# Routing attention and a mixer MLP: score groups of three key chunks instead of two, one PSUM bank for the small products

## The chip, the core and the metric

The kernel runs on one core of a Trainium2 chip. The metric is the device time of one execution in microseconds (us). The core's engines run side by side, each through its own list of instructions in order, and wait for each other by semaphores: TensorE (PE, matrix products; PEld is its weight load), VectorE (DVE), ScalarE (ACT), GpSimd (POOL) and SyncE (SP, which issues most DMA transfers). Products of PE land in PSUM, eight banks of 128 partitions by 2 KB (512 f32 numbers each); from there DVE or ACT reads them. SBUF is the larger working memory.

## The reference

What is computed, cut to what matters (B=4 batches, H=8 heads, S=768 positions, D=64, 16 clusters; the mixer has d_tok=256 and d_ch=1536):

```python
q_assign = argmax(einsum('bhsd,hcd->bhsc', q_n, c_n), axis=-1)
k_assign = argmax(einsum('bhsd,hcd->bhsc', k_n, c_n), axis=-1)
mask = q_assign[:, :, :, None] == k_assign[:, :, None, :]
scores = where(mask, scale * matmul(q, k.transpose(0, 1, 3, 2)), -1e9)
attn = exp(scores - max(scores, axis=-1, keepdims=True))
attn = attn / (sum(attn, axis=-1, keepdims=True) + 1e-09)
x = matmul(attn, v)                      # heads side by side: (B, S, 512)
h = maximum(x.transpose(0, 2, 1) @ w_tok1, 0) @ w_tok2
u = x + h.transpose(0, 2, 1)
out = u + maximum(u @ w_ch1, 0) @ w_ch2
```

`q_n`, `k_n` and `c_n` are the vectors divided by their norms.

## The kernel before

**Attention** works on pairs of heads: `NPAIR` = 16 pairs (batch b, heads 2f and 2f+1), counted by g. For one pair the 768 queries are two halves of 384 (`HS`, qh = 0, 1), and the 768 keys are six chunks of 128 (`NJ`). A group m is one half of the queries against two chunks of keys, so a pair has `GROUPS` = 6 groups and the loop at L745 runs over 96 of them, with five more iterations to drain. In the loop, `g, s = divmod(m, GROUPS)`: s is the place of the group within its pair.

For a group, `scores` (L352) computes for each chunk and each of the two heads a bf16 product of one-hot cluster vectors (`ohT`, which puts a large negative number where clusters differ) and adds the f32 product of keys and queries (`qkT`, the two halves of an f32 product are two instructions each). The two heads use two halves of the array's rows and run at the same time. One chunk fills a tile `sc` of two PSUM banks; ACT turns it into `ex` by an exponential (L367). `add_up` (L370) adds the `ex` tiles of a half on DVE into `sum`. `values` (L382) multiplies `ex` by the value vectors into `av` (one bank), and at the end of a half ACT copies it to `avT`.

Around them stand small products, all in tiles of the pool `ps_w` (three banks, tag "w"):

- `turn` (DVE transposes of the next pair's keys and queries into `qkT`), `route_products` (PE, `pr`), `route` (DVE: `sim`, `mx`, `oh`, in L310 to L316), and `route_turn` (PE transposes `po`, read by ACT into `ohT`): they prepare pair g+1 while pair g runs.
- `half_sums` (PE, `den`), `half_reciprocals` (DVE: `dent`, read from `den`, and `rcps`), `half_turn` (PE transposes `px` of `avT`) and `half_out` (DVE, reads `px` and writes `x`): they finish a half. They are issued 2, 3, 3 and 4 iterations after the half's last group.

The order of every engine's instructions is the order in which the program calls these functions; nothing reorders them. One iteration calls, in this order: `half_out` of group m-4, `add_up` of m-1, `scores` of m, `values` of m-2, one of the steps for the next pair (by s), the load of pair g+2 (s = 1), a weight step, `half_sums`, `half_reciprocals`, `half_turn`.

A **weight step** (`weight_steps`, L166) loads one piece of a weight matrix by SP, has ACT compute two helper tiles (`wh`, `wup`) of the piece before it and DVE and POOL round the one before that (L205 to L222). One is taken every `WEVERY` = 4 iterations.

**After attention** the token mixer (`tok1`, `tok2`, the list `ends`) and the channel mixer (`ch1_chunk`, `ch2_chunk`) run on PE nearly without a gap. The channel mixer keeps running products in PSUM tiles with the tags X and Z (`ps_m`, two buffers of each, opened where the score banks are closed) and Y (one tile of `ps_w`). `turn_u` (L526) transposes u for it, eight calls with four tiles `pt` of `ps_w`, each read by an ACT copy (L538). `fits` (L666) checks whether the fast path's assumptions hold; if not, `general` recomputes everything.

PSUM during attention: three banks `ps_w`, one `ps_av`, two tiles `sc` of two banks. Afterwards: three `ps_w`, one `ps_av`, four `ps_m`.

Of the kernel before, what the change touches and what calls it, by code (L numbers as in the profile page):

```python
# [17 lines left out]
C = 16  # L18
P = 128
# [11 lines left out]
QP = P // NQ  # L31
NPAIR = B * NF

GROUPS = NJ
WEVERY = 4
SM_SCALE = 0.125


# [8 lines left out]
def kernel(  # L47
# [35 lines left out]
    def pool(name, bufs, stack=None, **kw):  # L83
        return (stack or fast).enter_context(
            tc.tile_pool(name=name, bufs=bufs, reuse_waits="tile", **kw)
        )

    ps_w = pool("ps_w", 3, space=PSUM)
    ps_av = pool("ps_av", 1, space=PSUM)
    ps_sc_stack = fast.enter_context(ExitStack())  # L90
    ps_sc = pool("ps_sc", 2, ps_sc_stack, space=PSUM)

    xpool = pool("xpool", 1)
    wc1pool = pool("wc1pool", 1)
# [144 lines left out]
    def centroids_norm(cen):  # L239
        sq = rsmall.tile([P, D], F32, name="censq")  # L240
        ss = rsmall.tile([P, 1], F32, name="ss")
        nc.vector.tensor_tensor(out=sq, in0=cen, in1=cen, op=ALU.mult)
        nc.vector.reduce_sum(out=ss, in_=sq, axis=AX.X)

        lo = rsmall.tile([P, 1], F32, name="lo")
        nc.vector.tensor_scalar_max(out=lo, in0=ss, scalar1=float(2.0**-100))
        nrm = rsmall.tile([P, 1], F32, name="nrm0")
        nc.vector.tensor_scalar(
            out=nrm.bitcast(I32), in0=lo.bitcast(I32), scalar1=0.5, scalar2=float(0x1FBD1DF5),
            op0=ALU.mult, op1=ALU.add,  # L250
        )
        for it in range(3):
            rr = rsmall.tile([P, 1], F32, name="rr")
            nc.vector.reciprocal(out=rr, in_=nrm)
            tw = rsmall.tile([P, 1], F32, name="tw")
            nc.vector.scalar_tensor_tensor(
                out=tw, in0=ss, scalar=rr, in1=nrm, op0=ALU.mult, op1=ALU.add
            )
            nrm = rsmall.tile([P, 1], F32, name="nrm")
            nc.vector.tensor_scalar(  # L260
                out=nrm, in0=tw, scalar1=0.5, scalar2=(1e-6 if it == 2 else 0.0),
                op0=ALU.mult, op1=ALU.add,
            )
        rden = rsmall.tile([P, 1], F32, name="rden")
        nc.vector.reciprocal(out=rden, in_=nrm)
        cn = rsmall.tile([P, 2, D], F32, name="cn")
        for i in range(2):
            nc.vector.tensor_scalar_mul(out=cn[:, i], in0=cen, scalar1=rden)
        pc = ps_w.tile([P, H * C], F32, tag="w", name="pc")
        nc.tensor.transpose(out=pc, in_=cn.rearrange("p i d -> p (i d)"), identity=ident)  # L270
        nc.vector.tensor_copy(out=cnT, in_=pc)
        nc.vector.memset(cnd, 0.0)
        for i in range(2):
            rows = slice(i * D, (i + 1) * D)
            nc.vector.tensor_copy(
                out=cnd[rows, :, i], in_=cnT.rearrange("p (f i c) -> p f i c", f=NF, i=2)[rows, :, i]
            )


    def turn(g, kinds=(1, 0)):  # L280
# [3 lines left out]
        for a in kinds:  # L284
# [2 lines left out]
                in_=st["qk"][:, a].rearrange("p j i d -> p (j i d)"),  # L287
            )

    def route_products(g, a0=0, a1=2):  # L290

        st, f = state[g], g % NF
        pr = ps_w.tile([P, a1 - a0, NJ, QP], F32, tag="w", name="pr")
        for i in range(NQ):
            rows = slice(i * QP, (i + 1) * QP)
            nc.tensor.matmul(  # L296
                pr[rows], lhsT=cnd[:, f].rearrange("p i c -> p (i c)"),
                rhs=st["T"][:, a0:a1, :, rows].rearrange("p a j r -> p (a j) r"),
                start=True, stop=True,
            )  # L300
        st["pr"] = pr
# [20 lines left out]
    def route_turn(g, a):  # L322

        st, oh = state[g], ohs[g % 2]
        if a == 1:  # L330
            st["ohT"] = qktp.tile([P, 2, NJ, P], BF16, name="ohT")
        po = ps_w.tile([P, NJ, P], BF16, tag="w", name="po")
        for j in range(NJ):
            nc.tensor.transpose(out=po[:, j], in_=oh[:, a, j], identity=identb)  # L334
        if a == 0:
            if g == 0:
                nc.vector.tensor_copy(out=st["ohT"][:, 0], in_=po)  # L337
            else:
                nc.scalar.copy(out=st["ohT"][:, 0], in_=po)
        else:  # L340
            nc.scalar.activation(
                out=st["ohT"][:, 1], in_=po, func=ACT.Copy, scale=BIG, bias=-BIG,
                accum_out=cells[:, g : g + 1],
            )


    def split(m):

        g, s = divmod(m, GROUPS)
        return g, s // (GROUPS // 2), 2 * (s % (GROUPS // 2))  # L350

    def scores(m):  # L352
        g, qh, j0 = split(m)
        st = state[g]
        js = slice(HJ * qh, HJ * qh + HJ)
        scs = [ps_sc.tile([P, 2, 512], F32, name="sc") for _ in range(2)]
        for src, start in ((st["ohT"], True), (st["T"], False)):
            for i in range(2):
                for h in range(2):
                    rows = slice(h * D, (h + 1) * D)  # L360
                    nc.tensor.matmul(  # L361
                        scs[i][:, h, 0:HS], lhsT=src[rows, 1, j0 + i], rhs=src[rows, 0, js],
                        start=start, stop=not start,
                    )
        for i in range(2):
            ex = work.tile([P, 2, HS], F32, name="ex")
            nc.scalar.activation(out=ex, in_=scs[i][:, :, 0:HS], func=ACT.Exp, scale=SM_SCALE)  # L367
            st["ex", qh, j0 + i] = ex

    def add_up(m):  # L370
        g, qh, j0 = split(m)
        st = state[g]
        e = [st["ex", qh, j0 + i] for i in range(2)]
        if j0 == 0:
            acc = st["sum", qh] = sums.tile([P, 2, HS], F32, name="sum")
            nc.vector.tensor_tensor(out=acc, in0=e[0], in1=e[1], op=ALU.add)
        else:
            acc = st["sum", qh]
            for i in range(2):
                nc.vector.tensor_tensor(out=acc, in0=acc, in1=e[i], op=ALU.add)  # L380

    def values(m):  # L382
        g, qh, j0 = split(m)
        st = state[g]
        if j0 == 0:
            st["av"] = ps_av.tile([P, HS], F32, name="av")
        for j in (j0, j0 + 1):
            ex = st.pop(("ex", qh, j))
            for h in range(2):
                nc.tensor.matmul(  # L390
                    st["av"][h * D : (h + 1) * D], lhsT=st["va"][:, h, j], rhs=ex[:, h],
                    start=(j == 0), stop=(j == NJ - 1),
                )
        if j0 == NJ - 2:
            st["avT", qh] = sums.tile([P, HJ, P], F32, name="avT")
            nc.scalar.copy(out=st["avT", qh].rearrange("p j t -> p (j t)"), in_=st.pop("av"))

# [128 lines left out]
    def turn_u(b, n):  # L526
# [3 lines left out]
            pools["uTs"] = pools["u"].tile([P, 3, NF // 2, HS], F32, name="uTs")  # L530
        uT, uTs = pools["uT"], pools["uTs"]
        for f in range(NF):
            pt = ps_w.tile([P, HJ, P], F32, tag="w", name="pt")
            for i in range(HJ):
                nc.tensor.transpose(  # L535
                    out=pt[:, i], in_=xs[b][:, HJ * n + i, f * P : (f + 1) * P], identity=ident
# [14 lines left out]
    def chunk(n, product, done):  # L551


        def ptile(tag):
            if tag == "Y":
                return ps_w.tile([P, n], F32, tag="w", name="pY")
            return pools["ps_m"].tile([P, n], F32, tag=tag, name="p" + tag)

        X = ptile("X")
# [182 lines left out]

        return m // HALF if 0 <= m < last and m % HALF == HALF - 1 else None

    for m in range(last + 5):  # L745
        g, s = divmod(m, GROUPS)
        if half_at(m - 4) is not None:
            half_out(half_at(m - 4))
        if 1 <= m <= last:
            add_up(m - 1)  # L750
        if m < last:
            scores(m)
        if m == last:
            ps_sc_stack.close()
        if 2 <= m < last + 2:
            values(m - 2)
        if g < NPAIR - 1:
            if s == 0:
                turn(g + 1)
            elif s == 1:  # L760
                route_products(g + 1)
            elif s == 2:
                route(g + 1)
            elif s == 3:
                route_turn(g + 1, 1)
            elif s == 4:
                route_turn(g + 1, 0)
        if s == 1 and g + 2 < NPAIR:
            load(g + 2)
        if m == last - GROUPS:  # L770
# [1 line left out]
            routing.close()  # L772
            W["ch2"] = pool("wc2pool", 1, side="right").tile([P, NCT, DM], F32, name="wc2")
            weights = list(weight_steps(stage, W, ("ch2",)))
        if (m % WEVERY == 0 if m < last - GROUPS else m % 2 or m > last) and weights:
            weights.pop(0)()
        if half_at(m - 2) is not None:
            half_sums(half_at(m - 2))
        if half_at(m - 3) is not None:
            half_reciprocals(half_at(m - 3))  # L780
            half_turn(half_at(m - 3))
        if m >= last:
            if m == last:
                pools["ps_m"] = pool("ps_m", 2, space=PSUM)
            for _ in range(2):
                if ends:
                    ends.pop(0)()
    assert not state
    attention.close()
    pools["wsums"] = pool("wsums", 1, side="right")  # L790
# [238 lines left out]
```

## Time and profile before

| | us |
|---|---|
| median of 4 runs | 915.97 |
| the runs | 915.4 to 917.05 |
| the profiled execution | 915.2 |
| its span, first to last instruction | 913.4 |
| first `sc` block begins at | 14.68 |
| last pair of heads begins at | 347.74 |
| channel mixer begins at | 457.86 |

| stretch (us) | PE busy | DVE busy | ACT busy | granted clock |
|---|---|---|---|---|
| 34.3 to 347.7, pairs 2 to 15 | 313.40 | 242.79 | 182.53 | 1.00 |
| 368.6 to 457.9, token mixer | 89.30 | 51.38 | 18.71 | 1.00 |
| 457.9 to 913.4, channel mixer | 445.81 | 178.93 | 79.19 | 0.99 |

The profile is one execution. A group line has the source line, the engine, the operation, the tile written and the tiles read, how many there were, and then busy time, mean length of one, and idle time ahead of them with what ended it. In a timeline, each row has the start and the length in us of a run of like instructions, and in brackets how long the engine had been idle and what released it. Ends of matmuls are modelled, and consecutive ones overlap.

### The profile page before, as it was taken

How to read it: one execution, taken by the hardware profiler on the slowest of the kernel's cores; microseconds unless marked ns; L12 is line 12 of the kernel's file. 1: busy time of each engine (PE TensorE's matmuls, PEld its weight loads, DVE VectorE, ACT ScalarE, POOL GpSimd, SP SyncE). 2: the span in 40 equal slices, each digit the busy share in tenths (PEclk: the TensorE clock that was granted, in tenths of full speed). 3: DMA queues.
4: the chain of work that ended last, by engine and by line, in shares of the span. 5: the costliest groups of instructions: out<-in, count | busy, mean ns of one | idle time of the engine just before them, and what ended most of it. 6: DMA issues, size and time to landing. Idle time of an engine off the chain costs nothing.

```text
span 913.4 us, 11598 instructions
## 1 busy us (share of the span) xinstructions
PE 899.0 (98%) x4594; PEld 527.7 (58%) x4594; DVE 506.2 (55%) x851; ACT 307.2 (34%) x515; POOL 48.5 (5%) x40
## 2 busy tenths in 40 slices
PE   7999999999999999999999899999999999999997
PEld 3444444444444444444457668677686876858676
DVE  6778777878787765358554244343443334433342
ACT  3655565656565555232120021211212112130210
POOL 1011000101010100123000000000000000000000
PEclk9999999999999999999999999999999999999999
DMA  9553435353534200122000001000010000100001
GB/s 162 117 100 64 98 84 100 82 95 86 92 89 70 88 1 1 47 92 70 0 1 0 1 0 47 24 1 1 0 47 24 0 1 5 54 12 1 1 12 61
DMA packets 112830, 41.76 MB, mean 46 GB/s; under 512 B 101632, under 2 KB 105728, under 8 KB 112768
## 3 DMA queue, kind: packets, MB, share of 16 engines
q1 hardware_dynamic: 109632, 40.55, 19.5%
q10 hardware_dynamic: 3136, 0.39, 0.3%
q8 instruction: 38, 0.62, 0.3%
q14 instruction: 24, 0.20, 0.1%
HBM read 34.64 MB, written 6.29 MB: 45 GB/s over the span
## 4 chain that ended last, share of the span: by engine, by line
PE 98%; DMA 1%; DVE 0%; issue 0%; ACT 0%
PE sc L361 18%; PE av L390 15%; PE pX L596 14%; PE pX L647 14%; PE pZ L647 7%; PE pZ L596 7%; PE ph L463 5%; PE pu L472 5%; PE pY L647 3%; PE pY L596 3%; PE px L425 2%; PE po L334 2%; PE pr L296 1%; PE den L406 1%; PE pt L535 1%; DMA qk<-in_k_dram 1%
## 5 line engine op out<-in xcount | busy, mean ns | idle before, releaser
L367 ACT ACTIVATE ex<-sc 128x768 f32<-128x768 f32 x192 | 145.2, 808 | 116.5 <-PE sc L361 116.5
L380 DVE TENSOR_TENSOR sum<-sum,ex 128x768 f32<-128x768 f32 x128 | 132.9, 1038 | 31.1 <-ACT ex L367 22.6
L390 PE MATMUL av<-ex,va 128*64 128x384 f32 x768 | 145.1, 499 | 0.0
L361 PE MATMUL sc<-qkT 64*128 64x384 f32 x768 | 139.5, 482 | 0.0
L390 PEld LDWEIGHTS av<-ex,va 128*64 128x64 f32 x768 | 46.6, 136 | 86.5 <-issue 82.7
L361 PEld LDWEIGHTS sc<-qkT 64*128 64x128 f32 x768 | 70.5, 187 | 31.4
L596 PE MATMUL pX<-uT,wc 128*128 128x384 f32 x192 | 68.8, 495 | 1.6 <-issue 1.6
L604 ACT COPY p<-pX 128x384 f32<-128x384 f32 x24 | 11.4, 475 | 153.0 <-PE pX L596 153.0
L596 PEld LDWEIGHTS pX<-uT,wc 128*128 128x128 f32 x192 | 36.7, 193 | 26.7 <-issue 3.3
L361 PE MATMUL sc<-ohT 64*128 64x384 bf16 x384 | 48.2, 328 | 1.3 <-DVE ohT L337 0.6
L222 POOL TENSOR_TENSOR wc<-wT,wup 128x512 int32<-128x512 int32 x24 | 35.2, 1468 | 257.6 <-DVE wT L215 149.0
L431 DVE TENSOR_TENSOR x<-px,rcps 128x384 f32<-128x384 f32 x32 | 17.8, 558 | 47.9 <-PE px L425 46.7
L463 PE MATMUL ph<-x,wt 128*128 128x512 f32 x96 | 42.1, 594 | 0.0
L472 PE MATMUL pu<-h,wt 128*128 128x512 f32 x96 | 42.0, 592 | 0.0
L489 DVE TENSOR_TENSOR x<-pX,x 128x256 f32<-128x256 f32 x24 | 10.2, 424 | 53.0 <-PE pX L647 53.0
L489 DVE TENSOR_TENSOR c<-pZ,u 128x384 f32<-128x384 f32 x24 | 13.4, 558 | 46.8 <-PE pZ L596 46.8
L647 PE MATMUL pX<-w2s,hA 128*128 128x256 f32 x144 | 35.4, 382 | 0.5 <-DVE x L489 0.5
L489 DVE TENSOR_TENSOR hA<-pY,p 128x384 f32<-128x384 f32 x24 | 13.4, 557 | 40.4 <-PE pY L596 40.4
L647 PE MATMUL pX<-wc,hA 128*128 128x256 f32 x144 | 35.0, 379 | 0.0
L647 PE MATMUL pZ<-w2s,hS 128*128 128x256 f32 x144 | 35.0, 379 | 0.0
L647 PE MATMUL pY<-wc,hA 128*128 128x256 f32 x144 | 35.0, 379 | 0.0
L647 PE MATMUL pX<-w2s,hS 128*128 128x256 f32 x144 | 35.0, 379 | 0.0
(115 smaller groups left out, 1218.8 us busy)
## 6 DMA issues: line engine op xcount, KB each, us to landing
raw<-in_moe_w_ch_dram SPq DMA_DIRECT2D x24, 512.0 KB, 4.1
qk<-in_k_dram SPq DMA_DIRECT2D x64, 96.0 KB, 4.5
va<-in_v_dram SPq DMA_DIRECT2D x16, 384.0 KB, 3.3
out_dram<-x SPq DMA_DIRECT2D x24, 256.0 KB, 2.0
qk<-in_q_dram SPq DMA_DIRECT2D x60, 96.0 KB, 3.6
raw<-in_moe_w_tok_dram SPq DMA_DIRECT2D x3, 512.0 KB, 5.7
raw<-in_moe_w_tok_dram SPq DMA_DIRECT2D x4, 384.0 KB, 3.8
qk<-in_q_dram ACTq DMA_DIRECT2D x4, 96.0 KB, 4.3
```

The source lines that it names most:

```text
L222: nc.gpsimd.tensor_tensor(out=dst.bitcast(I32), in0=T, in1=up, op=ALU.add)
L334: nc.tensor.transpose(out=po[:, j], in_=oh[:, a, j], identity=identb)
L361: nc.tensor.matmul(scs[i][:, h, 0:HS], lhsT=src[rows, 1, j0 + i], rhs=src[rows, 0, js], start=start, stop=not start,)
L367: nc.scalar.activation(out=ex, in_=scs[i][:, :, 0:HS], func=ACT.Exp, scale=SM_SCALE)
L380: nc.vector.tensor_tensor(out=acc, in0=acc, in1=e[i], op=ALU.add)
L390: nc.tensor.matmul(st["av"][h * D : (h + 1) * D], lhsT=st["va"][:, h, j], rhs=ex[:, h], start=(j == 0), stop=(j == NJ - 1),)
L425: nc.tensor.transpose(out=px[:, i], in_=avT[:, i], identity=ident)
L463: nc.tensor.matmul(pf, lhsT=W["tok1"][:, j, t * P : (t + 1) * P], rhs=xs[b][:, j], start=(j == 0), stop=(j == NJ - 1),)
L472: nc.tensor.matmul(pu, lhsT=W["tok2"][:, t, j], rhs=h1s[b][:, t], start=(t == 0), stop=(t == NT - 1))
L489: nc.vector.tensor_tensor(out=dst, in0=a, in1=b, op=ALU.add)
L596: nc.tensor.matmul(psum, lhsT=A[a][:, k, c * P : (c + 1) * P], rhs=R[r][:, k], start=start and k == 0, stop=k == 1, skip_group_check=not s ...
L647: nc.tensor.matmul(psum, lhsT=h2[a][:, k, i * P : (i + 1) * P], rhs=Bw[w][:, 3 * part + k], start=start and k == 0, stop=k == 2, skip_grou ...
```

## The change

Groups have three chunks of keys (`NG` = 3), so a pair has four groups and the loop 64, with three iterations to drain. The score tiles take three times two banks; `ps_w` has one bank, which all small products share, apart from those of the first pair (`wtile` with g = 0) and `pc`, which use score tiles. `values` runs one group behind `scores` instead of two. The order in the loop is new, a weight step comes every third iteration, and after attention the tiles `pt` and `pY` are in `ps_m` with the tag Y (two buffers). In an iteration, `half_sums` and the first `route_turn` stand between `scores` and `values`; `half_turn`, `route_products` and the second `route_turn` stand behind `values`; `turn` and `route` come ahead of `add_up`. The helper `wtile` is called only by `route_products` and `route_turn`.

```diff
-GROUPS = NJ
-WEVERY = 4
+NG = 3
+GROUPS = 2 * NJ // NG
+WEVERY = 3
...
-    ps_w = pool("ps_w", 3, space=PSUM)
+    ps_w = pool("ps_w", 1, space=PSUM)
     ps_av = pool("ps_av", 1, space=PSUM)
     ps_sc_stack = fast.enter_context(ExitStack())
-    ps_sc = pool("ps_sc", 2, ps_sc_stack, space=PSUM)
+    ps_sc = pool("ps_sc", NG, ps_sc_stack, space=PSUM)
...
+    def wtile(g, shape, dt, name):
+
+        if g == 0:
+            return ps_sc.tile(shape, dt, tag="sc", name=name)
+        return ps_w.tile(shape, dt, tag="w", name=name)
...
-        scs = [ps_sc.tile([P, 2, 512], F32, name="sc") for _ in range(2)]
+        scs = [ps_sc.tile([P, 2, 512], F32, tag="sc", name="sc") for _ in range(NG)]
         for src, start in ((st["ohT"], True), (st["T"], False)):
-            for i in range(2):
+            for i in range(NG):
...
         if j0 == 0:
             acc = st["sum", qh] = sums.tile([P, 2, HS], F32, name="sum")
             nc.vector.tensor_tensor(out=acc, in0=e[0], in1=e[1], op=ALU.add)
-        else:
-            acc = st["sum", qh]
-            for i in range(2):
-                nc.vector.tensor_tensor(out=acc, in0=acc, in1=e[i], op=ALU.add)
+            e = e[2:]
+        acc = st["sum", qh]
+        for ex in e:
+            nc.vector.tensor_tensor(out=acc, in0=acc, in1=ex, op=ALU.add)
...
-        for j in (j0, j0 + 1):
+        for j in range(j0, j0 + NG):
...
-            pt = ps_w.tile([P, HJ, P], F32, tag="w", name="pt")
+            pt = pools["ps_m"].tile([P, HJ, P], F32, tag="Y", name="pt")
...
         def ptile(tag):
-            if tag == "Y":
-                return ps_w.tile([P, n], F32, tag="w", name="pY")
             return pools["ps_m"].tile([P, n], F32, tag=tag, name="p" + tag)
...
-    for m in range(last + 5):
+    for m in range(last + 3):
         g, s = divmod(m, GROUPS)
-        if half_at(m - 4) is not None:
-            half_out(half_at(m - 4))
+        more = g < NPAIR - 1
+        if half_at(m - 3) is not None:
+            half_out(half_at(m - 3))
+        if more and s == 0:
+            turn(g + 1)
+        if more and s == 1:
+            route(g + 1)
         if 1 <= m <= last:
             add_up(m - 1)
         if m < last:
             scores(m)
         if m == last:
             ps_sc_stack.close()
-        if 2 <= m < last + 2:
-            values(m - 2)
-        if g < NPAIR - 1:
-            if s == 0:
-                turn(g + 1)
-            elif s == 1:
-                route_products(g + 1)
-            elif s == 2:
-                route(g + 1)
-            elif s == 3:
-                route_turn(g + 1, 1)
-            elif s == 4:
-                route_turn(g + 1, 0)
+            pools["ps_m"] = pool("ps_m", 2, space=PSUM)
+        if half_at(m - 2) is not None:
+            half_sums(half_at(m - 2))
+            half_reciprocals(half_at(m - 2))
+        if more and s == 2:
+            route_turn(g + 1, 1)
+        if 1 <= m <= last:
+            values(m - 1)
+        if half_at(m - 2) is not None:
+            half_turn(half_at(m - 2))
+        if more and s == 0:
+            route_products(g + 1)
+        if more and s == 2:
+            route_turn(g + 1, 0)
         if s == 1 and g + 2 < NPAIR:
             load(g + 2)
...
-        if (m % WEVERY == 0 if m < last - GROUPS else m % 2 or m > last) and weights:
+        if m < last - GROUPS:
+            n = m % WEVERY == 0 or m == 1
+        else:
+            n = m % 2 if m < last else 2
+        for _ in range(min(n, len(weights))):
             weights.pop(0)()
-        if half_at(m - 2) is not None:
-            half_sums(half_at(m - 2))
-        if half_at(m - 3) is not None:
-            half_reciprocals(half_at(m - 3))
-            half_turn(half_at(m - 3))
         if m >= last:
-            if m == last:
-                pools["ps_m"] = pool("ps_m", 2, space=PSUM)
-            for _ in range(2):
-                if ends:
-                    ends.pop(0)()
+            for _ in range(3):
+                ends.pop(0)()
```

More of the change, by code (lines that the diff above doesn't have):

```diff
@@ L268, in centroids_norm @@
             nc.vector.tensor_scalar_mul(out=cn[:, i], in0=cen, scalar1=rden)
-        pc = ps_w.tile([P, H * C], F32, tag="w", name="pc")
+        pc = ps_sc.tile([P, H * C], F32, tag="sc", name="pc")
         nc.tensor.transpose(out=pc, in_=cn.rearrange("p i d -> p (i d)"), identity=ident)
@@ L288, in turn @@
             )
+    def wtile(g, shape, dt, name):
+        if g == 0:
+            return ps_sc.tile(shape, dt, tag="sc", name=name)
+        return ps_w.tile(shape, dt, tag="w", name=name)
     def route_products(g, a0=0, a1=2):
         st, f = state[g], g % NF
-        pr = ps_w.tile([P, a1 - a0, NJ, QP], F32, tag="w", name="pr")
+        pr = wtile(g, [P, a1 - a0, NJ, QP], F32, "pr")
         for i in range(NQ):
@@ L331, in route_turn @@
             st["ohT"] = qktp.tile([P, 2, NJ, P], BF16, name="ohT")
-        po = ps_w.tile([P, NJ, P], BF16, tag="w", name="po")
+        po = wtile(g, [P, NJ, P], BF16, "po")
         for j in range(NJ):
@@ L349, in split @@
         g, s = divmod(m, GROUPS)
-        return g, s // (GROUPS // 2), 2 * (s % (GROUPS // 2))
+        return g, s // (GROUPS // 2), NG * (s % (GROUPS // 2))
     def scores(m):
@@ L364, in scores @@
                     )
-        for i in range(2):
+        for i in range(NG):
             ex = work.tile([P, 2, HS], F32, name="ex")
@@ L372, in add_up @@
         st = state[g]
-        e = [st["ex", qh, j0 + i] for i in range(2)]
+        e = [st["ex", qh, j0 + i] for i in range(NG)]
         if j0 == 0:
@@ L376, in add_up @@
             nc.vector.tensor_tensor(out=acc, in0=e[0], in1=e[1], op=ALU.add)
-        else:
-            acc = st["sum", qh]
-            for i in range(2):
-                nc.vector.tensor_tensor(out=acc, in0=acc, in1=e[i], op=ALU.add)
+            e = e[2:]
+        acc = st["sum", qh]
+        for ex in e:
+            nc.vector.tensor_tensor(out=acc, in0=acc, in1=ex, op=ALU.add)
     def values(m):
@@ L393, in values @@
                 )
-        if j0 == NJ - 2:
+        if j0 == NJ - NG:
             st["avT", qh] = sums.tile([P, HJ, P], F32, name="avT")
```

## The prediction, made before the changed kernel was run

> **What bounds it now.** I read the page's busy shares first, then the chain of work that ended last, then the timeline of TensorE (PE) over one pair of heads, and only then VectorE (DVE), which releases most of what PE could wait for.
>
> ```profile
> PE 899.0 (98%) x4594; PEld 527.7 (58%) x4594; DVE 506.2 (55%) x851; ACT 307.2 (34%) x515; POOL 48.5 (5%) x40
> PE 98%; DMA 1%; DVE 0%; issue 0%; ACT 0%
> ```
>
> PE is never idle for long, and the chain is PE. So time changes only if PE's blocks become shorter or PE starts to wait. A busy PE is not PE at its peak, so the second look is at where blocks begin (columns: start, length, work; a length overlaps the next start, so I count start to start).
>
> ```profile
> 153.69 0.50 PE L361 MATMUL sc<-ohT 64*128 64x384 bf16 x4
> 154.02 1.45 PE L361 MATMUL sc<-qkT 64*128 64x384 f32 x8
> 155.41 1.51 PE L390 MATMUL av<-ex,va 128*64 128x384 f32 x8
> 156.85 0.55 PE L425 MATMUL px<-ident,avT 128*128 128x128 f32 x3
> 157.33 0.50 PE L361 MATMUL sc<-ohT 64*128 64x384 bf16 x4
> ...
> 174.97 0.85 PE L296 MATMUL pr<-qkT,cnd 128*32 128x384 f32 x8
> 175.63 0.51 PE L406 MATMUL den<-sum,ones 128*32 128x192 f32 x8
> 176.07 0.34 PE L361 MATMUL sc<-ohT 64*128 64x384 bf16 x2
> ```
>
> From 153.69 to 176.07 is one pair: 22.38 us. A block of sc takes 0.335 + 1.385, one of av 1.44. Four 384-column f32 matmuls whose shape doesn't change start 1.29 apart in all (457.86 to 459.15 in the timeline, product pX), 0.3225 each; sc and av hold four such slots each (two heads run side by side), so av pays 0.15 and sc 0.095 for the change of shape around them. That is what larger groups pay less often.
>
> **The change on PE, block by block.** A third chunk adds one bf16 slot (half of 0.335, so 0.165) and two f32 slots (0.645) to sc, and 0.645 to av: 0.50 + 2.03 and 2.09. A pair then has four of each in place of six: ohT 2.00 for 2.01, qkT 8.12 for 8.31, av 8.36 for 8.65. The small products stay seven: today pr 0.66, den 0.44 behind pr and 0.47 elsewhere, po twice 0.44, px twice 0.48, 3.41 in all. Now pr stands between av and sc; the one place where it runs into sc today is the start:
>
> ```profile
> 18.99 0.85 PE L296 MATMUL pr<-qkT,cnd 128*32 128x384 f32 x8
> 19.77 0.34 PE L361 MATMUL sc<-ohT 64*128 64x384 bf16 x2
> ```
>
> 0.78; with den twice 0.465, 3.55. Sum 22.03. Not shown today are sc into den or po, and den or po into av, three joins a pair. Nearest rows: sc into pr 1.40 (17.59 to 18.99) against 1.385 into av, so +0.015 each; the other bound is that they cost nothing. I take the lower middle, 22.04: 0.34 less per pair, ends 0.32 and 0.37. For pairs 2 to 15, 14 x 0.34 = 4.76.
>
> First pair, today 14.68 to 34.32, 19.64, with 0.25 and 0.36 lost to the exponentials. After: sc, pr 3.31; sc, av 4.62; sc, po, av, po 5.50; sc, den, av, px 5.57; sum 19.00, gain 0.64. Last pair, 347.74 to 368.59, 20.85: after 2 x 4.62 + 2 x 5.57 = 20.38, gain 0.47. Its tail: today av twice 1.44, den 0.46, px 0.33; after av 2.09, den, px. There den and px stand back to back in one bank, so px waits for the transpose dent behind a relu: 0.2 + 0.61 until DVE is free (the relu at 408.81 frees DVE at 409.42), 0.38, 0.05, so px starts 1.24 after den; 2.09 + 1.24 + 0.40 = 3.73, loss 0.06. Gain on PE 5.81, ends 5.2 and 6.5.
>
> **One bank for the small products.** Order on the bank: pr (s=0); den, px (s=1); po, po (s=2); den, px (s=3). Each waits for the reader of the one ahead. Readers on DVE run in order, so I lay DVE out from the start of sc at s=0, with these steps:
>
> ```profile
> 172.91 0.92 DVE L376 TENSOR_TENSOR sum<-ex 128x768 f32<-128x768 f32 x1
> 173.93 2.02 DVE L380 TENSOR_TENSOR sum<-sum,ex 128x768 f32<-128x768 f32 x2
> 175.88 0.58 DVE L310 STREAM_TRANSPOSE sim<-pr 128x384 f32<-128x384 f32 x1
> ...
> 177.57 0.42 DVE L205 TENSOR_SCALAR wh<-wh 128x512 f32<-128x512 f32 x1
> ...
> 179.16 0.38 DVE L411 STREAM_TRANSPOSE dent<-den 128x192 f32<-128x192 f32 x1
> ```
>
> Half_out starts 0.59 after px does (168.16 to 168.75), so at 0.11, and takes 0.47; turn 1.75 (171.15 to 172.91); three sums 2.98; DVE is free at 5.31. Pr starts at 0.50 + 2.03 + 2.09 = 4.62 and is done 0.90 later, so sim starts at 5.52; route 1.68 (175.88 to 177.57): 7.20; first sums 1.90: 9.10; dent ends 9.48. Px is due on PE at 5.40 + 0.50 + 2.03 + 0.47 + 2.09 = 10.49. Slack 0.96: no wait. The same way, po at s=2 is due 2 us after half_out, the second po 0.5 us after ScalarE's copy, px at s=3 1.5 us after dent. ACT's three exponentials end 3.6 us after their sc begins, and the next sc of that bank starts 4.6 us after at the earliest, so values one group behind cost nothing; without that cover each would cost up to one exponential, 0.81. The key and query loads of a pair now start at 4.7 us behind av of s=0 and took 12 us to issue and land (152.69 to about 165), against a need at 22.6; SP's weight loads queue among them, 0.4 each.
>
> Weight steps are what breaks the slack. One takes 1.59 on DVE (177.57 to 179.16), and its POOL addition holds up sums:
>
> ```profile
> 152.30 1.86 POOL L222 TENSOR_TENSOR wc<-wT,wup 128x512 int32<-128x512 int32 x1 [16.94 <-ACT ex L367]
> 153.13 2.91 DVE L380 TENSOR_TENSOR sum<-sum,ex 128x768 f32<-128x768 f32 x2
> ```
>
> 2.91 for two sums instead of 2.02. They come every third group, so at s=0 in every third pair: m = 12, 24, 36, 48. There sim starts at 6.90 and dent ends at 10.86 or, if oh is held up like a sum, 0.3 later: px 0.42 to 0.72 late. I take 0.6: 4 x 0.6 = 2.4. Steps at s=1, 2, 3 meet slack of 1 us or more. Behind the waiting px on PE is sc of s=2; nothing else is due.
>
> The Trainium skill (Perfetto Trace Analysis, "Matmuls") speaks against this part: independent groups should rotate through different banks so that evacuation overlaps the next group. By it, with no overlap, a pair would pay dent 0.38 and half_out 0.56 twice, sim 0.58 and two ohT copies of 0.8, an estimate of 4.1 us, or 62 us for 15 pairs. The rows put a 2.09 us av block between most users of the bank, and I count only where the sum above runs late.
>
> **Fewer banks after attention.** Transposes pt (turn_u) move from three banks to two.
>
> ```profile
> 553.01 1.61 PE L535 MATMUL pt<-ident,x 128*128 128x128 f32 x12
> 553.54 1.63 ACT L538 COPY uT<-pt 128x384 f32<-128x384 f32 x4 [6.31 <-PE pt L535]
> 554.07 0.31 PEld L535 LDWEIGHTS pt<-ident,x 128*128 128x128 f32 x3 [0.15 <-ACT uT L538]
> ```
>
> Four tiles, one ScalarE copy each; already the fourth tile waits until 554.07 for the first copy. With two banks the third does, and two tiles are left from 554.07, 0.39 + 0.33: pX starts at 554.79 instead of 554.46. 0.33 x 8 calls = 2.6; were ScalarE free earlier it couldn't be less than the first copy's end allows, so I give it 2.4 to 2.8. PY is read seven products before its bank returns: nothing.
>
> **Sum.** 5.8 - 2.6 - 2.4 = 0.8 us less. The profiled execution took 915.2 (span 913.4 and 1.8 around it), 0.77 under the median of 915.97; so 914.4 for one like it, 915.2 against the medians. The ends (gain 5.2 to 6.5, losses 4.1 to 5.7) give 913.6 to 916.5.
>
> **Rivals.**
> Hidden waits: the four late px vanish because sim starts before pr's modelled end or the addition doesn't slow oh, and the joins cost their low ends: 915.2 - 2.4 - 0.6 = 912.2. For it: DVE steps overlap by 0.08 in many rows. Against: 1.59 us of weight steps exceed the 0.96 of slack whatever POOL does.
>
> The bank chain late: pr, route, first sums, dent, px is one chain through a single bank from s=0 to s=1. If it runs 1.2 us later than laid out (a handover on each semaphore, a longer route), px waits 0.24 in the eleven pairs without weight steps at s=0 and 1.2 more in the four with them: 11 x 0.24 + 4 x 1.2 = 7.4, so 922.6, slower. It decides from 0.65 late on, since the four alone then cost 2.6 and bring 917.8. For it: DVE is busy 19.25 us of today's 22.38, so nothing late is caught up before s=3. Against: all its steps are in rows above.
>
> That the change doesn't do what it says: sc could be held by its own exponentials, as at 16.73 and 17.43 in the start today (0.25, 0.36); then 48 groups by 0.3 is 14 us, 930. Against: 1 us of room in the sum above.
>
> The clock: behind the check of fits, pX took 2.69 (515.17 to 517.86) where 1.29 is usual, PE having idled 1.91 and 1.64. Whether that recurs is worth 1.4 either way, inside the spread of 915.4 to 917.05. The Trainium skill (TensorE: Matmul & The Clock Gate, "A second HAM failure mode") would let small waits at PSUM banks drop the clock; by it each late px would cost such a stretch too, an estimate of 5.6. The waits of 0.25 and 0.36 at the start left the granted clock at 1.00.
>
> **Numbers.** Chances: forecast 0.55, hidden waits 0.25, late bank chain 0.16, held scores 0.04. About 0.2% (1.8 us) is what a measurement of this kernel tells from no change, 914.1 to 917.8; of the forecast's 0.55, 0.16 lies below it and 0.39 within. Faster 0.16 + 0.25 = 0.41, same 0.39, slower 0.20. I predict 915.1. The likeliest case's own range is 913.6 to 916.5; taking in the hidden waits and the near end of the late chain, 911.8 to 918.2.
>
> **What would show it.** A pair of 22.0 between starts of sc at s=0, with av blocks of 2.09: right about PE. Waits of px on dent in four pairs, 0.4 to 0.7 each; more pairs, and the late chain holds. The third pt tile waiting on ScalarE, pt blocks of 1.77 instead of 1.45. Waits of sc on exponentials would make the prediction wrong, as would a pair above 22.4.

## The result, and the profile after

| | before | after |
|---|---|---|
| median (us) | 915.59, 65 runs | 914.45, 44 runs |
| all runs | 914.1 to 917.54 | 911.71 to 916.25 |
| profiled execution, its span | 915.2, 913.4 | 915.41, 913.5 |
| first `sc` | 14.68 | 14.49 |
| first `ph` | 370.03 | 367.82 |
| first product of the channel mixer | 457.86 | 455.66 |

The ratio of after to before is 0.9988, 95% interval 0.9983 to 0.9993: 1.1 us less, between 0.6 and 1.6. The prediction was 915.1, by its sum 0.8 less than before. It started from 915.97, the median of the four executions known then; over 65 the median is 915.59, and 0.4 of the 0.65 by which the measured time lies under 915.1 comes from that.

The page's busy shares and its shares of the chain that ended last:

```profile
PE 894.0 (98%) x4594; PEld 533.0 (58%) x4594; DVE 507.4 (56%) x851; ACT 303.4 (33%) x515; POOL 45.0 (5%) x40
...
PE 92%; DVE 5%; DMA 1%; issue 1%; ACT 0%; DVEq 0%
```

PE is busy 5.0 us less for the same 4594 matmuls, and DVE has come into the chain with 5%: PE now waits for it in places. The view of PE's waits (who waits, for whom, us in total, times, longest) names them:

```profile
PE pr L303 <- DVE qkT L286: 2.5, 1, 2.5
PE px L432 <- DVE dent L418: 2.3, 4, 0.7
PE pt L542 <- ACT uT L545: 1.9, 8, 0.2
PE pn L688 <- DVE good L686: 1.9, 1, 1.9
```

The second and third are new: `px` waits three times in the loop and once in the drain, `pt` in each of the eight blocks. `pn` is as long as before, and `pr` comes back below. A stretch of PE's timeline over two groups with a weight step at s=0, and DVE's rows beside it:

```profile
148.04 2.16 PE L397 MATMUL av<-ex,va 128*64 128x384 f32 x12
150.13 0.85 PE L303 MATMUL pr<-qkT,cnd 128*32 128x384 f32 x8
150.91 0.66 PE L368 MATMUL sc<-ohT 64*128 64x384 bf16 x6
151.41 2.10 PE L368 MATMUL sc<-qkT 64*128 64x384 f32 x12
153.44 0.53 PE L413 MATMUL den<-sum,ones 128*32 128x192 f32 x8
153.90 2.16 PE L397 MATMUL av<-ex,va 128*64 128x384 f32 x12
156.60 0.55 PE L432 MATMUL px<-ident,avT 128*128 128x128 f32 x3 [0.54 <-DVE dent L418]
```

```profile
150.81 0.42 DVE L206 TENSOR_SCALAR wh<-wh 128x512 f32<-128x512 f32 x1
...
152.40 0.57 DVE L317 STREAM_TRANSPOSE sim<-pr 128x384 f32<-128x384 f32 x1
153.01 0.55 DVE L321 TENSOR_REDUCE mx<-sim 128x24 f32<-128x384 f32 x1
153.59 0.73 DVE L323 TENSOR_TENSOR oh<-sim,mx 128x384 bf16<-128x384 f32 x1
154.24 0.94 DVE L383 TENSOR_TENSOR sum<-ex 128x768 f32<-128x768 f32 x1
...
156.17 0.38 DVE L418 STREAM_TRANSPOSE dent<-den 128x192 f32<-128x192 f32 x1
...
173.66 0.58 DVE L317 STREAM_TRANSPOSE sim<-pr 128x384 f32<-128x384 f32 x1 [0.16 <-PE pr L303]
```

Blocks start 0.50, 2.03, 2.09 and 0.78 apart, and `den` is on the bank at 153.44. The last row is of the next pair, which has no step at s=0: there `sim` starts 0.92 after `pr` (172.74). Here that would be 151.05, but the three DVE operations of the weight step, from 150.81 on, hold `sim` until 152.40, and with it the sums and `dent`; `px`, due 2.09 after av at 155.99, starts at 156.60. From one pair's first `sc` to the next, pairs take 22.01, those with a step at s=0 22.19 (m = 12, whose piece is only 384 wide), 22.61, 22.61, 22.61: late by 0.18 (too little for the view of waits) and three times 0.61.

The transposes of u, with ScalarE's copies:

```profile
550.85 0.82 PE L542 MATMUL pt<-ident,x 128*128 128x128 f32 x6
551.38 0.86 ACT L545 COPY uT<-pt 128x384 f32<-128x384 f32 x2 [6.31 <-PE pt L542]
551.91 0.93 PE L542 MATMUL pt<-ident,x 128*128 128x128 f32 x6 [0.24 <-ACT uT L545]
552.68 0.38 PE L652 MATMUL pX<-wc,hA 128*128 128x256 f32 x1
```

Two tiles run, the third waits until 551.91 for the first copy, and the block takes 1.83 (550.85 to 552.68) where it took 1.45. The view counts 0.24 as idle, for it takes a matmul as busy to its modelled end; block lengths are what to add up.

The start of the profiled execution, PE's rows, and three stretches of it (the line has the stretch, its length, busy time of each engine, the granted clock, DMA share, GB/s):

```profile
14.49 1.15 PE L368 MATMUL sc<-ohT 64*128 64x384 bf16 x6 [0.65 <-DVE ohT L344]
15.40 3.52 PE L368 MATMUL sc<-qkT 64*128 64x384 f32 x12
18.85 0.85 PE L303 MATMUL pr<-qkT,cnd 128*32 128x384 f32 x8
```

```profile
0.00:14.40 14.40, 9.00 (x52) 4.23 (x53) 8.45 (x32) 2.41 (x4) 3.62 (x9) 0.90 1.01 140
14.40:18.90 4.50, 4.41 (x22) 2.47 (x24) 1.90 (x3) 1.48 (x2) 0.00 (x0) 0.57 0.99 264
18.90:30.00 11.10, 11.10 (x86) 5.17 (x86) 8.31 (x10) 7.81 (x14) 0.00 (x0) 1.00 0.94 209
```

The first `sc` group took 4.36 (14.49 to 18.85) at a granted clock of 0.57. In an execution at full clock (the second experiment) the same block took 2.58, from 14.56 to 17.14. So 1.8 us of this profiled execution belong to the clock at its start and hide the gain. Executions of both kernels differ in their clock: the mean granted clocks of after's lie at 0.998 with times around 913.8, or at 0.991 to 0.994 with mostly 915.3 to 916.3. A low mean doesn't say where the clock was low. The trace of the second experiment has 0.994 without a drop at the start: behind the check of `fits` its half clock lasts from 508.12 to 514.95, in after's trace from 513.17 to 516.58, and from `pn` to the last product it takes 397.90 where after takes 396.76, for the same instructions.

### The profile page after: what moved, and what is told of

Its sections match the earlier page's. It is cut to its first block, busy times and chain, and to the rows that moved or that the text cites. A ratio compares the mean times of both kernels' runs of the same rounds, so it can differ in the third digit from the quotient of the medians.

```text
span 913.5 us, 11630 instructions
## 1 busy us (share of the span) xinstructions
PE 894.0 (98%) x4594; PEld 533.0 (58%) x4594; DVE 507.4 (56%) x851; ACT 303.4 (33%) x515; POOL 45.0 (5%) x40
## 4 chain that ended last, share of the span: by engine, by line
PE 92%; DVE 5%; DMA 1%; issue 1%; ACT 0%; DVEq 0%
PE sc L368 16%; PE pX L601 14%; PE pX L652 14%; PE av L397 13%; PE pZ L652 7%; PE pZ L601 7%; PE ph L470 5%; PE pu L479 5%; PE pY L652 3%; PE pY L601 3%; PE px L432 2%; DVE sum L387 2%; PE po L341 2%; PE den L413 1%; PE pt L542 1%; PE pr L303 1%
## 5 line engine op out<-in xcount | busy, mean ns | idle before, releaser
L374 ACT ACTIVATE ex<-sc 128x768 f32<-128x768 f32 x192 | 141.8, 812 | 119.2 <-PE sc L368 119.2
L397 PE MATMUL av<-ex,va 128*64 128x384 f32 x768 | 138.0, 494 | 0.0
L387 DVE TENSOR_TENSOR sum<-sum,ex 128x768 f32<-128x768 f32 x128 | 130.2, 1017 | 10.1
L368 PE MATMUL sc<-qkT 64*128 64x384 f32 x768 | 135.7, 486 | 0.0
L397 PEld LDWEIGHTS av<-ex,va 128*64 128x64 f32 x768 | 49.4, 136 | 66.2 <-issue 59.2
L223 POOL TENSOR_TENSOR wc<-wT,wup 128x512 int32<-128x512 int32 x24 | 32.4, 1350 | 251.2 <-DVE wT L216 251.2
L368 PE MATMUL sc<-ohT 64*128 64x384 bf16 x384 | 42.8, 329 | 0.7 <-DVE ohT L344 0.7
```

Of the source, the lines that this page charges most:

```text
L223: nc.gpsimd.tensor_tensor(out=dst.bitcast(I32), in0=T, in1=up, op=ALU.add)
L368: nc.tensor.matmul(scs[i][:, h, 0:HS], lhsT=src[rows, 1, j0 + i], rhs=src[rows, 0, js], start=start, stop=not start,)
L387: nc.vector.tensor_tensor(out=acc, in0=acc, in1=ex, op=ALU.add)
L397: nc.tensor.matmul(st["av"][h * D : (h + 1) * D], lhsT=st["va"][:, h, j], rhs=ex[:, h], start=(j == 0), stop=(j == NJ - 1),)
```

## Experiments

**E1, transposes over four banks.**

```diff
-            pt = pools["ps_m"].tile([P, HJ, P], F32, tag="Y", name="pt")
+            pt = pools["ps_m"].tile([P, HJ, P], F32, tag="YYZZ"[f], name="pt")
```

> The changed kernel with the four tiles pt of a turn_u spread over two Y and two Z banks. Bank theory: the third tile no longer waits for a ScalarE copy, a block of twelve transposes falls from 1.83 us to about 1.37 (12 x 0.109 and the change of shape), so 8 x 0.45 = 3.6 us less than the changed kernel, about 911. Rival, ScalarE paces the transposes whatever the banks (its copies start 0.375 apart) and the wait only moves to the product behind them: pX starts no earlier, 914.5.

Measured 910.96 (910.8 to 912.46), ratio to before 0.9958 (0.9941 to 0.9974), 3.5 under after. Its timeline:

```profile
549.32 1.47 PE L542 MATMUL pt<-ident,x 128*128 128x128 f32 x12
549.85 1.63 ACT L545 COPY uT<-pt 128x384 f32<-128x384 f32 x4 [6.31 <-PE pt L542]
550.63 1.24 PE L652 MATMUL pX<-wc,hA 128*128 128x256 f32 x5
```

One row of twelve without a break, 1.31 to pX; ScalarE's copies end after pX has begun and nobody waits for them. The loss was the banks'; the rival falls. By the blocks it is 6 x 0.52 + 2 x 0.49 = 4.1, the two being those in the token mixer (1.82 and 1.33); that the medians show 3.5 may be the clock, for this trace too has the long half clock behind `fits` (508.91 to 515.74).

**E2 and E3, where the weight steps stand.** The changed kernel has them at every third group. E2 takes them out of s=0, E3 puts one at s=0 of fourteen pairs; both have 21 steps.

```diff
-            n = m % WEVERY == 0 or m == 1
+            n = s == 3 or (s == 1 and g < 6)                                # E2
+            n = m < 2 or (s == 0 and g >= 1) or (s == 3 and g < 5)          # E3
```

> The changed kernel with no weight step at s=0: one at s=3 of every pair and one at s=1 of the first six pairs, 21 as before. Theory of the late bank chain in four pairs: the four waits of px for dent (2.3 us in all) vanish and nothing replaces them, 2.3 us less than the changed kernel, about 912.2. Rival, DVE is short of time as such and the same wait comes up at another place (half_out, sums, den): 914.5 with waits elsewhere on PE.

> The changed kernel with a weight step at s=0 in fourteen pairs instead of four (and at m=0, m=1 and at s=3 of the first five pairs, 21 in all). Theory: px waits about 0.6 in each of the fourteen, 8.2 us instead of 2.3, so 5.9 more than the changed kernel, about 920.3. Rival, the four waits come from something else at m=12, 24, 36, 48 (a late transfer, POOL): no more than the four, 914.5.

E2: 912.85 (911.82 to 913.75), ratio 0.9970 (0.9961 to 0.9980), 1.6 under after by the medians where 2.3 was expected. From the second to the fifteenth all pairs take 22.01, which is 2.0 less than in after. E3: 920.36 (919.27 to 921.02), ratio 1.0054 (1.0037 to 1.0071), 5.9 over after. The same line of the view of PE's waits, first E2, then E3:

```profile
PE px L432 <- DVE dent L418: 0.7, 1, 0.7
```

```profile
PE px L432 <- DVE dent L418: 7.1, 13, 0.7
```

In E2 one wait is left, that of the drain, and no new line stands in the view. In E3 fourteen pairs are late, by 0.54, 0.18, 0.18 and eleven times 0.61, 7.6 in all (the view leaves out the two small ones and has the one of the drain). The waits follow the steps, one for one.

**E4, more changes of shape and no other work.** The first chunk of `values` stands between the second and third chunk of the next group's scores.

```diff
         for src, start in ((st["ohT"], True), (st["T"], False)):
             for i in range(NG):
+                if not start and i == NG - 1 and m >= 1:
+                    values(m - 1, 0, 1)
```

> The changed kernel with values of each group cut in two: its first chunk is multiplied between the second and third chunk of the next group's scores, so every group has two more changes of shape on PE and no other work. Theory, the gain per pair is changes of shape saved: 0.25 us for each added visit to av (3.16 for today's plain group of two less 2 x 0.165 and 8 x 0.3225), 63 groups, 15.8 us more, about 930. Rival, the gain per pair is fewer waits between engines: no waits are added here, so within 1 us of 914.5.

Measured 934.83 (two runs, 934.09 and 935.57), ratio 1.0213 (1.0193 to 1.0233), 20.4 over after. Its timeline of PE:

```profile
151.97 0.66 PE L370 MATMUL sc<-ohT 64*128 64x384 bf16 x6
152.47 1.45 PE L370 MATMUL sc<-qkT 64*128 64x384 f32 x8
153.86 0.87 PE L399 MATMUL av<-ex,va 128*64 128x384 f32 x4
154.65 0.92 PE L370 MATMUL sc<-qkT 64*128 64x384 f32 x4
155.50 1.51 PE L399 MATMUL av<-ex,va 128*64 128x384 f32 x8
156.94 0.53 PE L303 MATMUL pr<-qkT,cnd 128*32 128x384 f32 x4
```

From 152.47 to 156.94 it is 4.47 for the work that takes 2.03 + 2.09 = 4.12 undivided: 0.35 for each added visit, 22.1 for 63. As every group is longer, DVE catches up and the four late `px` are gone, 2.0; 20.1 is left, and 20.4 was measured. Visits cost time though PE waits for nobody more than before, which rules out the rival: fewer visits are the gain of the larger groups. That the price is one of shape, and not of any new block, is read from the prediction's rows of before: `pr` runs 0.66 into `den`, of the same shape 128*32, and 0.78 into sc. The size was off: I had 0.25. The visit to av costs the 0.15 foreseen (two slots of 0.3225 in 0.79). But the second part of sc takes 0.85 for two slots, 0.20 over, not 0.095: there PE comes from av straight into f32 scores, while a normal group comes into the bf16 product first, whose start costs 0.01.

**E6, both mends**, the edits of E1 and E2 together.

> The changed kernel with both mends: tiles pt over two Y and two Z banks, no weight step at s=0. Theory, the two losses are separate: 911.0 (pt alone) less the 2.0 us of px waits, 909.0, that is 6.6 under the kernel before. Rival, they overlap, or one mend shifts the clock drops: 910.5 or more.

Measured 908.14 (906.49 to 909.27), ratio 0.9915 (0.9900 to 0.9931): 7.8 under before, 6.3 under after, and 0.9 under the 909.0 expected. The losses were separate. Its trace and that of before can be compared as they are: neither has the drop at the start, both have 3.41 us of half clock behind `fits`, and the spans are 905.9 and 913.4, 7.6 apart.

**E7 and E8, the transposes alone, in the kernel before.** E7 gives `pt` two banks, E8 four (a Z tile for the last).

```diff
-            pt = ps_w.tile([P, HJ, P], F32, tag="w", name="pt")
+            pt = pools["ps_m"].tile([P, HJ, P], F32, tag="Z", name="pt")    # E7
+            pt = (ps_w.tile([P, HJ, P], F32, tag="w", name="pt") if f < 3   # E8
+                  else pools["ps_m"].tile([P, HJ, P], F32, tag="Z", name="pt"))
```

> The kernel before with one part of the change alone: pt on two banks (the Z tiles) instead of three. Theory: a block of transposes takes 1.83 instead of 1.45, eight blocks, 3.0 us more than before, 918.6. Rival, in the kernel before a wait there is covered: 915.6.

> The kernel before with a fourth bank for pt (the last tile goes to a Z tile). Theory: blocks of 1.31 instead of 1.45, 8 x 0.135 = 1.1 us less than before, 914.5; set against the changed kernel with both mends it leaves the groups of three alone, 5.5 us. Rival, nothing: 915.6.

E7: 920.56 (919.81 to 921.6), ratio 1.0053 (1.0038 to 1.0069), 4.6 over the 915.94 of before on that chip, not 3.0. PE's waits tell why:

```profile
PE pt L535 <- ACT uT L538: 1.9, 8, 0.2
...
PE pt L535 <- DVE x L475: 0.9, 2, 0.5
```

Six blocks take 1.83 as foreseen. The two in the token mixer take 2.45, because its products use the Z tiles too and DVE's addition still reads one: 6 x 0.38 + 2 x 1.0 = 4.3. That loss is the experiment's own; with Y tiles, as in the changed kernel, it doesn't occur. E8: all eight blocks take 1.31. The time is 915.47 (912.1 to 916.27), ratio 0.9987 (0.9975 to 0.9999): 1.2 less by the ratio, between 0.1 and 2.3, and 0.5 less by the medians. The 1.1 expected lies within, but six of its ten executions had a mean clock of 0.992 to 0.994, so its time settles no more than the sign, and the difference from E6 isn't used.

**E9, px of the drain behind the token products**; E6 with this besides.

```diff
-        if half_at(m - 2) is not None:
+        if half_at(m - 2) is not None and m < last:
             half_turn(half_at(m - 2))
...
             for _ in range(3):
                 ends.pop(0)()
+            if half_at(m - 2) is not None:
+                half_turn(half_at(m - 2))
```

> Both mends, and behind the last group px stands after the three token products instead of straight behind den. Theory: the one wait of px left (0.77 us of den to px) goes and nothing takes its place, 0.8 under both mends alone (908.1), 907.3. Rival, the saved wait comes back where the token products wait for DVE: 908.1.

Measured 908.07 (906.73 to 909.3), ratio 0.9913 (0.9898 to 0.9927). In the traces the wait is gone: after's drain, then E9's:

```profile
383.46 0.53 PE L413 MATMUL den<-sum,ones 128*32 128x192 f32 x8
384.70 0.52 PE L432 MATMUL px<-ident,avT 128*128 128x128 f32 x3 [0.70 <-DVE dent L418]
```

```profile
380.22 0.53 PE L413 MATMUL den<-sum,ones 128*32 128x192 f32 x8
380.68 5.42 PE L470 MATMUL ph<-x,wt 128*128 128x512 f32 x12
```

From the first `ph` to the channel mixer E9's trace takes 86.16, E6's 86.86: 0.7. The medians, 0.07 apart, can't show it over the spread of the start.

**E5 and E10, warming products.** E5 is the changed kernel with eleven warming products instead of seven ahead of the first `pr`. E10 is E9 with fourteen, and four ahead of the first scores.

```diff
-        keep_warm(7)
+        keep_warm(14)        # E10; 11 in E5
...
         route_turn(0, 0)
+        keep_warm(4)         # E10
```

> The changed kernel with four more warming products on PE ahead of the first pr (eleven instead of seven). Theory: in some executions PE idles 2.5 us before pr, the clock drops to one half and the first scores block takes 1.8 us longer; four more products cut the idle time by 0.65 (0.163 each at full clock), so drops get rarer and the median falls from 914.5 towards the 913.7 of executions without a drop. Rival, the drop is a matter of where a free-running window begins and four products change nothing: median 914.5, as wide a spread.

> The same with fourteen warming products instead of seven ahead of the first pr and four more ahead of the first scores. Theory, the clock drop at the start follows from PE idling there, and fuller warming stops it: no run with half the clock in the first 30 us, median 906.5 or less and a narrow spread. Rival, it hangs on the phase of a free-running window: as many drops, and where the clock is still low the products delay pr by up to 1 us, 907.3 to 908.

E5: 913.47 (911.96 to 915.7), ratio 0.9976 (0.9966 to 0.9987); its profiled execution had the half clock all the same (12.01 to 18.84), with PE idle 1.7 ahead of `pr`. Five of its eleven executions were above 913.8. Undecided. E10: 906.95 (906.27 to 907.38), ratio 0.9898 (0.9883 to 0.9914), the fastest version here. All four executions have a mean clock of 0.996 or more, where three of E9's six have 0.992; PE is without a gap over 0.4 us between 6.41 and the first scores. The median lies between the theory's 906.5 and the rival's 907.3 to 908. Four executions with a high clock fit the theory that idling at the start brings the drop, but four don't show that it is gone.

## Why the prediction was right

| step | foreseen | measured |
|---|---|---|
| a pair without a late `px` | 22.04 | 22.01 |
| first pair | 0.64 less | 0.6 less at full clock (E2; 0.66 in E1 and E6) |
| last pair | 0.47 less | 0.5 less |
| drain, `den` to `px` | 1.24 | 1.24 |
| late `px` | 4 x 0.6 = 2.4 | 0.18 + 3 x 0.61 = 2.0 |
| `pt` blocks | 8 x 0.33 = 2.6 | 8 x 0.38 = 3.0 |
| sum | 0.8 less | 1.1 less (0.6 to 1.6) |

**PE's blocks.** They came as added up: 0.50 + 2.03, 2.09, `pr` 0.785, `den` 0.46, `po` 0.44, `px` 0.48. The joins that no row of before showed (sc into den or po, and those into av) cost what other joins cost, 2.03, 0.46 and 2.09, so their low end was right; that is 14 x 0.03 of the difference. E4 shows that visits cost time without any wait, and gives the price of one more in the middle of f32 scores, 0.35.

**One bank.** The chain from `pr` over `route`, the first sums and `dent` to `px` has slack in every pair without a weight step at s=0 and none with one: E2 removes the waits with the steps, E3 multiplies them. The working came as laid out: `sim` was put 5.52 behind the pair's first sc and 6.90 with a step, and started at 5.53 and 6.88. The rule of the Trainium skill that was weighed against this part (Perfetto Trace Analysis, "Matmuls", rotate banks) holds for the places where no long block lies between two users: `den` and `px` of the drain (0.77), and the pt tiles. Elsewhere its 62 us did not come.

**Two banks for pt.** The mechanism was right and the size small: the third tile starts 0.05 after the first copy as said, but then tiles three and four took 0.77 (551.91 to 552.68), not the 0.72 taken from a block with one restart.

**What went against it.** Two points. I put whatever the clock does into the spread, and looked for it only behind the check of `fits`; the larger swing is at the start, 1.8 us (by the first pair 0.5 in E3's trace and 2.2 in E5's), and it decides whether one profiled execution of after lies over or under one of before. And of the rivals, hidden waits came in half, the joins at their low end, but the waits themselves didn't vanish; the late chain falls, for pairs without a step take 22.01; and held scores fall too: scores wait for no exponential in the view of PE's waits.

**Terms against medians.** The measured terms give 0.6 + 14 x 0.37 + 0.5 - 2.0 - 3.0 = 1.3 less, within the interval of 0.6 to 1.6. The traces give 1.5: from the first sc to the last product before takes 893.1 and after 893.4, of which 1.8 is the clock at the start. That the two losses came to the 5.0 foreseen is luck: `px` was 0.4 less and `pt` 0.4 more. And the interval is too wide to tell 0.8 from 1.3. E6 has neither loss, and its four banks shorten each `pt` block from 1.45 to 1.31: 6.3 + 8 x 0.135 = 7.4 under before by the terms, 7.6 by the traces, 7.8 by the medians.

## What to carry to other kernels

On a PE that never idles, count changes of array shape: fewer and longer visits of each shape save the price of a visit (here 0.15 for av and 0.095 for scores), which can be read off as start-to-start time less slots. The buffers that pay for longer visits are taken from someone: lay out each bank's users in order, with the reader between them, and find the one iteration in which the reader's engine also has extra work; move that work to another iteration before giving the buffer back. Where a profile of one execution and the medians disagree, compare the granted clock by stretch before explaining the work, and hold it against the length of a product that you know: ahead of 13.19 E2's granted clock reads 1.00, and its products there take the time of half the clock (below).

## What the runs showed of the hardware

- Coming into a block costs by the type of its first product: into bf16 scores 0.01 (0.50 for three slots of 0.163, as warming products follow each other at full clock), from av into f32 scores 0.11 (0.85 for two slots of 0.3225, less the 0.095 of leaving).
- The clock at the start halves in some executions only: granted 0.50 from 11.41 to 18.24 in after's profile, not in E2's. PE's rows ahead of it, after's and then E2's:

```profile
6.21 1.30 PE L719 MATMUL av<-warm 128*128 128x384 bf16 x7
9.97 0.53 PE L303 MATMUL pr<-qkT,cnd 128*32 128x192 f32 x8 [2.45 <-DVE qkT L286]
```

```profile
6.30 2.45 PE L719 MATMUL av<-warm 128*128 128x384 bf16 x7
10.01 0.87 PE L303 MATMUL pr<-qkT,cnd 128*32 128x192 f32 x8 [1.27 <-DVE qkT L286]
```

The same products take about twice as long in E2's: there the clock came up only behind them, and stayed; in after's it had come up before them, and fell back. So the 1.3 of idle time against 2.5 is in the main the slower warming products (2.45 against 1.30) and doesn't show that idling brings the drop. Of the twelve traces here, the four in which the granted clock is listed at full by 6 us (after, E3, E5, E8) fell back for 6.83 us; seven in which it is first listed between 13.2 and 14.1 didn't, and neither did E10, whose PE was kept busy (9.76). Which of the two decides, the early rise or the idling behind it, stays open. The Trainium skill (TensorE: Matmul & The Clock Gate, "What's actually happening") has a free-running activity window behind such drops. That would fit drops that come and go between executions of one kernel, and half clocks of 3.41 us (513.17 to 516.58 in after's) and of twice that; that such a window runs free, no run here shows. The late `px` of 0.6 us, against what I quoted as that page's other warning, left the granted clock at 1.00 from 35.3 to 344.
- POOL's addition of a weight step, 152.62 to 153.90, lay beside the first 0.31 us of the two-input operation `oh`, which took 0.73 instead of 0.56; in the kernel before it lay beside the two sums for 1.03 us, and they took 2.91 instead of 2.02. The one-input `mx` beside it took its usual 0.55.
